# Three weight tiles move from the last attention step to the output phase, and the fills there are dealt out anew

## The chip, the core and the metric

The kernel runs on one core of a Trainium2 chip. A core has TensorE (matrix products, called PE in the profile, with its weight loads as PEld), VectorE (DVE), ScalarE (ACT), GpSimd (POOL) and SyncE (SP), which run side by side and wait for each other through semaphores; 16 DMA engines move data between HBM and the on-chip memories SBUF and PSUM. The metric is the device time of one execution in microseconds (us). The kernel is measured in repeated runs, and the median counts. Before the change it is 441.6 us (ten runs, 441.0 to 442.49).

## What is computed

Two layers. The first is an attention with feature maps instead of a softmax; the second takes its output, mixes 64 low frequencies of the sequence with complex weights, transforms back and adds a ReLU layer. In the reference, cut to what matters:

```python
def _attn_ref(q, k, v, w_phi):            # q, k, v: (8, 8, 576, 64)
    def phi(x):
        proj = np.einsum('bhsd,df->bhsf', x, w_phi)
        proj = proj - np.max(np.abs(proj), axis=-1, keepdims=True)
        return np.concatenate([np.exp(proj), np.exp(-proj)], axis=-1)
    q_p, k_p = (phi(q), phi(k))
    kv = np.einsum('bhsf,bhsd->bhfd', k_p, v)
    z = np.sum(k_p, axis=2)
    num = np.einsum('bhsf,bhfd->bhsd', q_p, kv)
    den = np.einsum('bhsf,bhf->bhs', q_p, z)[..., None] + 1e-06
    return num / den

def _moe_ref(x, w_r, w_i, w_ch):          # x: (8, 576, 512), w_r, w_i: (64, 512, 512)
    X = np.fft.rfft(x, axis=1)
    Xr, Xi = (np.real(X[:, :64]), np.imag(X[:, :64]))
    Yr = np.einsum('bmd,mde->bme', Xr, w_r) - np.einsum('bmd,mde->bme', Xi, w_i)
    Yi = np.einsum('bmd,mde->bme', Xr, w_i) + np.einsum('bmd,mde->bme', Xi, w_r)
    Y = np.zeros_like(X); Y[:, :64] = Yr + 1j * Yi
    y = np.fft.irfft(Y, n=576, axis=1)
    u = x + y
    return u + np.maximum(u @ w_ch, 0.0)
```

The weights w_r and w_i are by far the largest input: 2 x 64 matrices of 512 x 512.

## The kernel before

**Tiling.** The attention is cut into 16 units, a unit being one pair of heads g (four of them) and one pair of batches bp (four). The 512 channels of the second layer are the same four groups g of 128. The frequency weights are cut into 64 tiles: a key (g, w) names channel group g, octet o = w // 2 (eight frequencies) and i = w % 2 (w_r or w_i). A tile is 128 partitions x 4 x 2 x 512 in bf16, 1 MB on the chip, converted from float32 by the DMA. Using a tile is called a mix (function `mix`, L461): eight matmuls of 512 columns into one PSUM bank. An octet is finished by its eighth mix, over the four groups and both kinds of weights.

**Weight tiles.** `next_w` (L359) takes the next key from the list and issues its load on POOL's queue. Most tiles lie in the pool `pw` with nine buffers; a tile that is issued has to wait for the buffer that a former mix gives back. In the output phase the same pool also gives the buffers of `yall` and `zall` (and later `yl`, `rx`, `of`), which are taken when they are first written.

**Attention loop.** It starts at L504 with n from -2 to 16. Step n runs the early stages of unit n + 1 and n + 2, the main stages of unit n (called Q) and the last stage, the Fourier sums, of unit n - 1 (called P). Between these stages `some` (L488) runs mixes whose tiles are due and issues a load after each. How many mixes a step runs follows from X at L506: none before step 4, eight in step 4, three in each later step. In the last step, n = 16, there is no unit 16: Q is None, P is unit 15, and the step consists of the Fourier sums of unit 15 and three mixes.

**Output phase.** It starts at L574. The mixes that are left run in the loop at L900, each followed by `next_w(1)`. Between them `fill(n)` (L797) takes n pieces of other work from the list `todo`: 37 pieces (one opening piece and 36 calls of `hold`) that transpose a 128-row chunk of the attention output and multiply it by w_ch (the last three of them leave the product open in PSUM), then six pieces that finish these three chunks, then 33 pieces (`all`) that add the inverse transform of octets 0 to 5 to a chunk and to its product. The first of these pieces also build tables for the inverse transform on DVE and ACT. The pieces from the 38th on need octets 0 to 5 in `yall` and `zall`; A at L795 is the number of such pieces. TensorE, DVE, ACT, POOL and SP each execute their instructions in the order of the program, so the order written in this loop is the order of execution on each engine.

**When an octet is done** (g = 3, i = 1, L913), DVE adds the bank to the sum in `yacc` and writes `yst`, SP stores it into `yall`, TensorE transposes `yst`, multiplies it by w_ch (`pz`), and the result goes as `zst` to `zall`. For octets 0 to 4 one or two fills lie between these steps; for octets 5 and later the fills come behind them. After octet 7, the last, the chunks are finished and stored (class `Last`, from L811).

**How fills are dealt out.** `left` is the number of mixes still to come, and n at L912 is computed after each mix. While more than seven are left, the pieces that don't need the stored octets are spread over the mixes until seven are left; from then on, all that is left is spread over the remaining mixes. Eight are left when octet 5, the sixth, is stored.

## Time and profile before

One execution was profiled. Its own time is 441.52 us and its span, from the first to the last instruction, 439.7 us.

| what | value |
|---|---|
| median of ten runs | 441.6 us |
| profiled execution, time / span | 441.52 / 439.7 us |
| PE busy | 337.5 us (77% of the span) |
| DVE busy | 297.9 us (68%) |
| ACT busy | 278.1 us (63%) |
| POOL busy | 97.0 us (22%) |
| HBM read / written | 163.64 MB / 9.44 MB |
| mean granted TensorE clock | 0.907 of full speed |

In order of time: the attention, with mixes strewn in, runs until about 286 us; the output phase's mixes and fills follow until 404 us, and the final matmuls and stores until the end. A line of TensorE's list in order of time reads: start in us, duration, engine, operation, the tile written <- the tiles read, the sizes, how many matmuls in a row, and in brackets how long the engine was idle before and whose event ended that. `wt,XT` are mixes, `wchb,xT` the products of fills, `ident_b,xs` their transposes. Page and tables give the clock as a share of full speed, and DMA as the mean busy share of the 16 engines, where packets that overlap can bring it above 1.

### The profile page before, as it was taken

How to read it: one execution, taken by the hardware profiler on the slowest of the kernel's cores; microseconds unless marked ns; L12 is line 12 of the kernel's file. 1: busy time of each engine (PE TensorE's matmuls, PEld its weight loads, DVE VectorE, ACT ScalarE, POOL GpSimd, SP SyncE). 2: the span in 40 equal slices, each digit the busy share in tenths (PEclk: the TensorE clock that was granted, in tenths of full speed). 3: DMA queues.
4: the chain of work that ended last, by engine and by line, in shares of the span. 5: the costliest groups of instructions: out<-in, count | busy, mean ns of one | idle time of the engine just before them, and what ended most of it. 6: DMA issues, size and time to landing. Idle time of an engine off the chain costs nothing.

```text
span 439.7 us, 10163 instructions
## 1 busy us (share of the span) xinstructions
PE 337.5 (77%) x4247; PEld 203.9 (46%) x4247; DVE 297.9 (68%) x583; ACT 278.1 (63%) x478; POOL 97.0 (22%) x138
## 2 busy tenths in 40 slices
PE   3667757869777687797796785927689988999993
PEld 2345545636555455464564463613345544344320
DVE  5768588676684777866878778717763433776694
ACT  4698698677798577865877777502544432656681
POOL 7132132132221222222222121211101120010171
PEclk9989699698899689886989789987899999999996
DMA  8999999999999999999999999999999999996797
GB/s 167 236 211 210 236 214 237 232 218 240 236 211 239 220 228 236 237 212 237 225 222 238 210 239 226 225 212 212 212 216 223 219 224 221 213 217 144 244 360 297
DMA packets 51582, 99.55 MB, mean 226 GB/s; under 512 B 2512, under 2 KB 13648, under 8 KB 51536
## 3 DMA queue, kind: packets, MB, share of 16 engines
q0 software_dynamic: 45376, 86.45, 99.8%
q1 hardware_dynamic: 6160, 12.45, 8.0%
q8 instruction: 33, 0.54, 0.5%
q14 instruction: 13, 0.11, 0.1%
HBM read 163.64 MB, written 9.44 MB: 394 GB/s over the span
## 4 chain that ended last, share of the span: by engine, by line
DMA 35%; PE 34%; DVE 13%; ACT 10%; issue 5%; POOL 1%; DVEq 0%; POOLq 0%; ACTq 0%
PE one L37 12%; PE pt L37 12%; DMA vn<-in_v_dram 11%; DMA kb<-in_k_dram 10%; DMA wt<-in_moe_w_i_dram 7%; DMA wt<-in_moe_w_r_dram 7%; PE two L37 6%; PE pp L37 5%; ACT AB L37 5%; DVE m L37 3%; DVE mk L37 3%; ACT AQ L37 2%; DVE xw L37 2%; DVE xs L37 2%; ACT qT L37 1%
## 5 line engine op out<-in xcount | busy, mean ns | idle before, releaser
L37 ACT ACTIVATE AB<-two 128x1024 bf16<-128x1024 f32 x64 | 62.0, 1026 | 17.1 <-DVE mk L37 14.6
L37 ACT ACTIVATE AQ<-two 128x1024 bf16<-128x1024 f32 x64 | 62.6, 1045 | 2.6 <-PE two L37 2.5
L37 ACT CAST xw<-pt 128x512 bf16<-128x512 f32 x50 | 29.4, 587 | 45.2 <-PE pt L37 30.8
L37 DVE TENSOR_REDUCE m<-two 128x8 f32<-128x1024 f32 x32 | 39.2, 1224 | 15.1 <-PE two L37 15.0
L37 DVE TENSOR_TENSOR va<-vn,ee 128x1152 bf16<-128x1152 f32 x32 | 42.0, 1355 | 5.5 <-DMA vn<-in_v_dram 5.5
L37 DVE TENSOR_REDUCE mk<-two 128x8 f32<-128x1024 f32 x32 | 38.9, 1218 | 7.1 <-PE two L37 7.1
L37 PE MATMUL pt<-wchb,xT 128*128 128x512 bf16 x136 | 37.0, 397 | 6.6 <-DVE xT L37 5.7
L37 POOL DMA_DIRECT2D wt<-in_moe_w_i_dram x28 | 20.9, 747 | 84.3 <-PE pt L37 38.2
L37 POOL DMA_DIRECT2D wt<-in_moe_w_r_dram x30 | 22.4, 746 | 76.2 <-PE one L37 34.7
L37 PEld LDWEIGHTS <-xs 128*128 128x128 bf16 x624 | 31.7, 103 | 12.7 <-issue 7.4
L37 PE MATMUL one<-wt,XT 128*32 128x512 bf16 x304 | 27.5, 446 | 12.9 <-DMA wt<-in_moe_w_i_dram 4.3
L37 ACT COPY qT<-one 128x512 bf16<-128x512 bf16 (+1 forms) x32 | 19.3, 641 | 27.5 <-PE one L37 27.1
L37 PE MATMUL two<-w2blk,qT 128*128 128x256 bf16 x128 | 22.7, 307 | 18.0 <-ACT AB L37 8.9
L37 PEld LDWEIGHTS <-qT 128*128 128x128 bf16 x144 | 14.9, 106 | 36.5 <-issue 32.9
L37 PE MATMUL two<-qT,w2blk 128*128 128x512 bf16 x64 | 27.7, 432 | 3.5 <-ACT AQ L37 3.4
L37 PEld LDWEIGHTS <-XT 128*32 128x32 bf16 x512 | 14.7, 149 | 32.6 <-issue 16.8
L37 DVE RECIPROCAL rd<-one 128x6 f32<-128x6 f32 x48 | 9.4, 195 | 28.5 <-PE one L37 28.4
L37 PEld LDWEIGHTS <-AQ 128*128 128x128 bf16 x512 | 24.9, 109 | 7.9 <-issue 4.4
L37 PE MATMUL one<-kvz,AQ 128*128 128x65 bf16 x512 | 27.6, 209 | 1.1 <-ACT qT L37 1.0
L37 DVE TENSOR_TENSOR xs<-one,rd 128x384 bf16<-128x384 f32 x48 | 26.8, 558 | 1.6
L37 PE MATMUL two<-mT,minus 96*128 96x512 bf16 x64 | 27.5, 430 | 0.2 <-DVE mT L37 0.2
L37 PE MATMUL two<-w2blk,kT 128*128 128x256 bf16 x128 | 21.2, 294 | 8.2 <-ACT AB L37 8.2
(147 smaller groups left out, 712.4 us busy)
## 6 DMA issues: line engine op xcount, KB each, us to landing
wt<-in_moe_w_r_dram POOLq DMA_DIRECT2D x30, 1024.0 KB, 28.4
wt<-in_moe_w_i_dram POOLq DMA_DIRECT2D x28, 1024.0 KB, 29.0
vn<-in_v_dram POOLq DMA_DIRECT2D x15, 576.0 KB, 25.0
out_dram<-of SPq DMA_DIRECT2D x16, 512.0 KB, 4.6
kb<-in_k_dram POOLq DMA_DIRECT2D x16, 288.0 KB, 22.1
qb<-in_q_dram POOLq DMA_DIRECT2D x16, 288.0 KB, 21.6
xs<-in_moe_w_i_dram POOLq DMA_DIRECT2D x2, 1024.0 KB, 24.8
yacc<-in_moe_w_r_dram POOLq DMA_DIRECT2D x1, 1024.0 KB, 9.8
```

The lines of the kernel that those rows point to most:

```text
L37: ins = f(*args, **kwargs)
```

## The change

The last attention step runs no mixes any more: X becomes 0 where there is no unit Q. The three mixes, (2, 8), (2, 9) and (2, 10), are left in the list and run as the first ones of the output phase, each followed by its `next_w(1)` as before, and now with fills behind them. Their results go to a bank of the output phase's pool instead of one of the attention's.

The rule for n changes too: while more than eight mixes are left, the pieces that don't need stored octets, less four, are spread over the mixes until eight are left; when exactly eight are left, which is when the sixth octet is stored, n is four; below eight it is the old formula.

```diff
-        X = 0 if n < 4 else 6 if n == 4 else 3
+        X = 0 if n < 4 or not Q else 6 if n == 4 else 3
...
         left = len(mixq)
-        n = -(-max(len(todo) - A, 0) // (left - 7)) if left > 7 else math.ceil(len(todo) / (left - 0.4)) if left else 0
+        if left > 8:
+            n = -(-max(len(todo) - A - 4, 0) // (left - 8))
+        else:
+            n = 4 if left == 8 else math.ceil(len(todo) / (left - 0.4)) if left else 0
```

Fills per mix, as the two rules give them. Mixes are numbered 1 to 64 in the order in which they run; the mix in bold stores an octet.

| mix | 41, 42, 43 | 44, 45, **46** | 47 to **50** | 51, **52** | 53 to 55 | **56** | 57, 58, 59, **60**, 61, 62, 63 |
|---|---|---|---|---|---|---|---|
| before | none | 3 each | 3 each | 3, 2 | 2 each | 2 | 7, 7, 7, 6, 6, 6, 3 |
| after | 2 each | 2 each | 2 each | 2 each | 2 each | 4 | 7, 7, 7, 6, 6, 6, 3 |

(48 and 54 store octets as well.)

## The prediction

> **What bounds the kernel now.** I read the first page, then a table of the stretches after the attention, then TensorE in order of time from 285 us, then the weight issues on POOL's queue. I number the 64 weight tiles, and the mix that uses each, in the order of their loads: mix 44 is the first mix of the output phase before the change, mix 56 ends the sixth octet, mix 64 ends the eighth.

> ```profile
> span 439.7 us, 10163 instructions
> ...
> q0 software_dynamic: 45376, 86.45, 99.8%
> ```

> The queue that carries the weights fills the 16 engines over the whole span. The next view is a table by stretch (engine busy times, then TensorE's clock, the DMA share, GB/s):

> ```profile
> 287.00:298.00 11.00, 2.45 (x32) 0.80 (x23) 1.59 (x4) 0.53 (x2) 1.52 (x3) 0.76 1.12 212
> 298.00:321.00 23.00, 17.85 (x128) 9.56 (x120) 18.01 (x72) 10.43 (x18) 2.92 (x4) 0.82 1.12 212
> 321.00:361.00 40.00, 36.90 (x306) 19.63 (x305) 18.00 (x48) 17.06 (x33) 5.18 (x7) 1.00 1.12 221
> 361.00:378.00 17.00, 14.55 (x103) 6.88 (x102) 8.17 (x16) 5.91 (x12) 1.48 (x2) 1.00 1.12 219
> 378.00:404.00 26.00, 25.14 (x151) 9.96 (x144) 19.65 (x33) 16.13 (x31) 2.14 (x4) 1.00 1.03 204
> ```

> The DMA share is 1.12 in every stretch up to 378 us; TensorE is idle for most of 287 to 298 and all but full from 321. In TensorE's order of time (start, duration, idle before and what ended it):

> ```profile
> 292.52 1.02 PE L37 MATMUL one<-wt,XT 128*32 128x512 bf16 x8 [4.25 <-DMA wt<-in_moe_w_r_dram]
> 297.48 1.08 PE L37 MATMUL one<-wt,XT 128*32 128x512 bf16 x8 [3.93 <-DMA wt<-in_moe_w_i_dram]
> ...
> 299.99 1.89 PE L37 MATMUL pt<-wchb,xT 128*128 128x512 bf16 x4 [0.46 <-DVE xT L37]
> ...
> 361.43 0.66 PE L37 MATMUL pt<-wt,XT 128*32 128x512 bf16 x8 [0.86 <-DMA wt<-in_moe_w_i_dram]
> ...
> 364.53 1.03 PE L37 MATMUL pt<-wchb,xT 128*128 128x512 bf16 x4
> ...
> 366.80 0.66 PE L37 MATMUL pt<-wt,XT 128*32 128x512 bf16 x8 [0.16 <-DMA wt<-in_moe_w_r_dram]
> ...
> 372.62 0.67 PE L37 MATMUL pt<-wt,XT 128*32 128x512 bf16 x8 [0.29 <-DMA wt<-in_moe_w_i_dram]
> ...
> 377.57 0.66 PE L37 MATMUL pt<-wt,XT 128*32 128x512 bf16 x8 [0.24 <-DMA wt<-in_moe_w_r_dram]
> ...
> 403.60 0.66 PE L37 MATMUL pt<-wt,XT 128*32 128x512 bf16 x8
> ```

> Mixes 42, 43 and 44 (287.61, 292.52, 297.48) wait 0.37, 4.25 and 3.93 us for their weights: 8.55 us of TensorE. Then TensorE is behind until mix 56 at 361.43, which again waits for weights, as do 57, 58 and 59, each by less than a microsecond. From 377.57 the chain of waits runs on TensorE to mix 64 at 403.60 without a gap. The weights are there just as late: POOL's queue shows

> ```profile
> 333.68 0.74 POOL L37 DMA_DIRECT2D wt<-in_moe_w_i_dram  x1 [18.19 <-PE pt L37]
> ...
> 367.78 0.74 POOL L37 DMA_DIRECT2D wt<-in_moe_w_i_dram  x1 [4.64 <-PE pt L37]
> ```

> These are loads 56 and 64; the list of issues gives 27.7 and 35.5 us to landing, so they land at 361.4 and 403.3. Two equally long paths thus meet at mix 64: the DMA queue, and from mix 57 on TensorE. After it the tail of 439.7 - 403.6 = 36.1 us follows.

> [...] weights move at 212 GB/s in 298 to 321, and when SP's stores of octets join, the sum is only 221. So the order in which the two queues are fed doesn't create bandwidth. [...] two neighbouring windows in the table by stretch:

> ```profile
> 306.34:309.76 3.42, 1.40 (x12) 0.78 (x11) 2.85 (x5) 2.96 (x4) 0.74 (x1) 1.00 1.12 211
> 309.76:313.17 3.41, 3.16 (x14) 1.59 (x13) 2.31 (x5) 1.20 (x3) 0.00 (x0) 0.50 1.13 212
> ```

> A window with TensorE busy 1.40 of 3.42 us (41%) is followed by one at 0.50; the product at 299.99, in another such window, took 1.89 us against 1.03 at 364.53. The window at 361 with 2.20 of 3.40 (65%) is followed by a full one. [...]

> **The change part by part.** (1) X = 0 in the last step takes mixes 41 to 43 out of it; they come before mix 44 in the output phase. Nothing is added or dropped: 3 x 8 matmuls, three loads on POOL (loads 50 to 52), one sum into yacc on DVE move with them. The instruction order of POOL and of SP is the same as before, and so are the tiles that each load waits for: loads 50 to 55 wait for the mix nine before, from 56 on for the mix seven before, because yall and zall then hold two of the nine buffers. Load 56 waited for mix 49 before (332.70, issue 333.68) and does after.

> (2) Fills (here each a product with its transposes, plus a piece of the table building on DVE) that stood behind mixes 44 to 46 three at a time now stand behind 41 to 46 two at a time. So TensorE, which slept 8.55 us, works. It is then ahead: two products take 2 x 1.08 = 2.16 us (365.39 to 364.31 is 1.08 from one to the next), a mix 0.66, half an octet's own work about 0.75 (an estimate: some 1.5 us of TensorE between 362.62 and 364.31), together 3.6 us beside one load in 361.43 - 355.9 = 5.5 us (load 55: 314.74 + 41.2 = 355.9) or 5.0 when weights move alone. By mix 53 at the latest TensorE waits for every tile. What is this worth? Nothing at mix 56: before, it already waited there for load 56, whose landing the saturated queue sets. Load issue isn't late either: load 56 found 3 to 4 others outstanding (loads 52 to 55) and can only be issued earlier.

> (3) Up to the sixth octet 32 fills were done before mix 56 and two behind it; after, 30 before and four behind it. From mix 57 on both are the same: 42 fills left, 7, 7, 7, 6, 6, 6 and 3. So between mix 56, fixed by load 56, and mix 57 TensorE has two more products: +2.16 us. What lay free there: 0.16 us of waiting at mix 57, then 0.29 at 58 and 0.24 at 59, which the delay eats: 0.69. The waits for yst (0.53) and yT (0.19) in the octet are before the products and stay. Net 2.16 - 0.69 = 1.47 us at mix 59. From there to 403.60 TensorE has no waits that a delay can eat, and the loads 60 to 64 land earlier than needed. So mix 64 starts at 403.60 + 1.47 = 405.07, and the tail moves with it: all of it hangs on the last octet's yst, whose matmuls and DVE adds follow at once.

> (4) Small: octet 4's stores, 2 x 128 KB, were under way when load 56 landed (issues at 354.77 and 358.28, 6.4 us to land); after, they come about 4 us earlier and are through. At most half of the second, 64 KB at 212 GB/s or 0.3 us, moves ahead of load 56 and delays it; load 57 has the same bytes before it. I take 0.1, keep 0 to 0.3.

> (5) Not visible before: the clock. After mix 55 at about 356, TensorE works 0.66 + 2.16 = 2.8 us and then waits some 2.6 us for load 56. [...] If that one falls on the octet and its four products, work of up to 1.7 us becomes 3.4: between 0 and +1.7 us, by where the free windows lie; a cold window that begins before 361 covers the wait and the octet's latency-bound part, and costs less. Before, this place was safe (3.07 of 3.50 us busy in 357.5 to 361.0). The stretch from mix 57 is dense, so only one window counts. As the likeliest I take +0.4, since more than half of the positions meet the products with part of a window or none; ends 0 and 1.7.

> Sum: 1.47 + 0.1 + 0.4 = +2.0 us. Profiled: 439.7 + 2.0 = 441.7 us of span; the profiled execution's time was 441.52, and the median of the ten runs 441.6, so 441.6 + 2.0 = 443.6.

> **The rivals.** (A) Two products too many behind octet six, as above: 443.6, own range 442.7 to 445.0. For it: four mixes in a row that wait for DMA by under 0.9 us, then none that waits.

> (B) No change. The two products cost less than counted, because something else between mixes 57 and 59 gives way: for example the 0.56 us wait at 371.60 for the DVE sum into xs, or the yall landing (issue 362.92 + 6.4 = 369.3, 1.1 us ahead of its first use at 370.44), so that 2.16 - 0.69 - 0.56 = 0.9 us or less is left, and the clock stays warm: 441.6 to 442.4. Against it: that 0.56 is a wait for a PSUM bank whose releaser stands right behind on the same engines, so it moves along.

> (C) Faster: the loads land sooner. Place: the queue between 287 and 361; if its 74 us ran at 221 GB/s rather than 212 in the first 34 (octet stores begin at about 313, not 322, and deeper queues), 34 x 9 / 212 = 1.4 us; it decides only if load 56 lands more than 1.6 us sooner, since the products' delay comes off it. Were the whole stretch 4% faster, 3.0 us, mix 64 would be at 403.60 - 3.0 + 2.0 = 402.6, and the time 440.6. Against it: bytes and engines are the same, and the rate was 212 with eight loads outstanding and with four.

> (D) Much slower: cold windows repeat, since in each 5 us TensorE now waits 1 to 2.4 us from mix 45 to 56, and the first fills come while the last attention step still holds banks. The work before mix 56 has about 1.4 us of slack per load, so this shows only if it reaches mix 56 itself: a full cold window there, and one behind mix 57, about +3.5: 445.1 and more.

> **How the numbers follow.** A change of 0.2% (0.9 us) is about what a measurement of this kernel can tell from none. Chances: A 0.62, B 0.22, C 0.08, D 0.08. A's lower end at 442.7 is slower by 0.25%, so slower = A + D = 0.70; B is the same but for some of it, 0.20 after 0.02 goes to faster; faster 0.10. The likeliest, A, gives 443.6. The range leaves out C and the far part of D and of B: 441.5 to 445.0.

> **What would show it.** Right: no waits for weights left between 287 and 298 without products beside them; mix 56 at 361.4 to 361.7 after a wait of over 2 us; four products behind octet six; mix 57 at 368.7 or later with no wait for its load; mixes 58 to 64 without waits, 64 at about 405.5; a tail of 36.1 us. A clock of 0.5 in one window near 361 would add to it. Wrong: mix 56 before 360, which makes the DMA queue elastic (C); mix 57 within 0.9 us of 366.80 (B); a TensorE that still runs late at mix 56, without a wait, which would break step 2.

## The result, and the profile after

The changed kernel takes 445.12 us in the median of 12 runs, against 441.75 us of the kernel before in 42 runs alongside it: a ratio of 1.0075 with a 95% interval of 1.0064 to 1.0086. That is 3.4 us slower. The profiled execution took 445.37 us, with a span of 443.6 us, 3.9 us more than before.

TensorE's list in order of time, after the change (start, duration, idle before and what ended it):

```profile
287.10 0.62 PE L37 MATMUL pt<-ident_b,xs 128*128 128x128 bf16 x8
...
290.25 0.66 PE L37 MATMUL pt<-wt,XT 128*32 128x512 bf16 x8
...
355.73 0.66 PE L37 MATMUL pt<-wt,XT 128*32 128x512 bf16 x8 [0.93 <-DMA wt<-in_moe_w_r_dram]
...
361.83 1.08 PE L37 MATMUL pt<-wt,XT 128*32 128x512 bf16 x8 [3.17 <-DMA wt<-in_moe_w_i_dram]
...
364.35 1.89 PE L37 MATMUL pt<-wchb,yT 128*128 128x256 bf16 x8 [0.19 <-ACT yT L37]
...
366.46 1.91 PE L37 MATMUL pt<-wchb,xT 128*128 128x512 bf16 x4
...
369.61 1.03 PE L37 MATMUL pt<-wchb,xT 128*128 128x512 bf16 x4
...
371.65 0.66 PE L37 MATMUL pt<-wt,XT 128*32 128x512 bf16 x8
...
377.11 0.66 PE L37 MATMUL pt<-wt,XT 128*32 128x512 bf16 x8
...
381.88 0.66 PE L37 MATMUL pt<-wt,XT 128*32 128x512 bf16 x8
...
407.89 0.67 PE L37 MATMUL pt<-wt,XT 128*32 128x512 bf16 x8
```

The waits for weights between mixes 42 and 44 are gone: transposes and products stand there from 287.10 (with two waits for DVE, of 1.35 us and, while it builds tables, of 3.27 us). Read on to mix 56: it starts at 361.83, after 3.17 us of waiting for its weights, 0.40 us later than before (361.43), so the early work bought nothing. Then comes what costs: mix 57 starts at 371.65, against 366.80. From mix 56 to mix 57 it was 5.37 us and is 9.82 us. The waits that stood before mixes 57, 58 and 59 are gone, so 4.85 us of delay at mix 57 are 4.49 at 58 (377.11 against 372.62), 4.31 at 59 (381.88 against 377.57) and 4.29 at mix 64 (407.89 against 403.60). What follows mix 64 takes 443.6 - 407.9 = 35.7 us, against 36.1 before.

The operations in that stretch are longer, too: the mix 1.08 us and not 0.66, the first product 1.91 and not 1.03. In the profiles before and after, every stretch between two changes of the clock is a multiple of 3.41 us; a piece of that length is called a window here. The table by stretch of the changed kernel, with the four windows around mix 56 (window, length, then busy time of PE, PEld, DVE, ACT, POOL, TensorE's clock, DMA share, GB/s):

```profile
354.77:358.18 3.41, 2.48 (x24) 1.36 (x24) 1.19 (x3) 0.83 (x2) 0.74 (x1) 1.00 1.12 223
358.18:361.59 3.41, 0.48 (x3) 0.13 (x1) 0.08 (x1) 0.61 (x2) 0.00 (x0) 1.00 1.12 223
361.59:365.00 3.41, 2.45 (x16) 0.93 (x16) 1.05 (x3) 0.37 (x1) 0.74 (x1) 0.50 1.13 213
365.00:368.42 3.42, 3.42 (x17) 2.00 (x16) 0.80 (x2) 0.38 (x2) 0.00 (x0) 0.50 1.11 216
```

The wait fills the second window (0.48 of 3.41 us busy), and the third and fourth run at half clock (0.50). The DMA share is 1.11 to 1.13 in all four: the queue of weights does not run dry here, and it is TensorE that arrives late at mix 64. Load 64 is issued at 372.62 and lands 30.4 us later, at 403.0, nearly 5 us before it is used.

### The profile page after: what moved, and what is told of

It is laid out like the page before. It is cut to its first block, busy times and chain, and to the rows that moved or that the text cites. A ratio compares the mean times of both kernels' runs of the same rounds, so it can differ in the third digit from the quotient of the medians.

```text
span 443.6 us, 10168 instructions
## 1 busy us (share of the span) xinstructions
PE 342.1 (77%) x4247; PEld 205.6 (46%) x4247; DVE 298.6 (67%) x583; ACT 278.3 (63%) x478; POOL 97.1 (22%) x138
## 3 DMA queue, kind: packets, MB, share of 16 engines
q0 software_dynamic: 45376, 86.45, 98.9%
## 5 line engine op out<-in xcount | busy, mean ns | idle before, releaser
L37 ACT ACTIVATE AB<-two 128x1024 bf16<-128x1024 f32 x64 | 62.0, 1026 | 12.3 <-DVE mk L37 9.8
L37 ACT ACTIVATE AQ<-two 128x1024 bf16<-128x1024 f32 x64 | 62.7, 1045 | 2.6 <-PE two L37 2.5
L37 ACT CAST xw<-pt 128x512 bf16<-128x512 f32 x50 | 29.4, 588 | 47.0 <-PE pt L37 44.2
L37 DVE TENSOR_REDUCE m<-two 128x8 f32<-128x1024 f32 x32 | 39.2, 1224 | 17.7 <-PE two L37 17.7
L37 PE MATMUL pt<-wchb,xT 128*128 128x512 bf16 x136 | 38.4, 408 | 9.4 <-DVE xT L37 8.5
L37 DVE TENSOR_TENSOR va<-vn,ee 128x1152 bf16<-128x1152 f32 x32 | 42.0, 1355 | 3.1 <-DMA vn<-in_v_dram 3.1
L37 DVE TENSOR_REDUCE mk<-two 128x8 f32<-128x1024 f32 x32 | 38.9, 1218 | 7.6 <-PE two L37 7.6
L37 POOL DMA_DIRECT2D wt<-in_moe_w_i_dram x28 | 21.1, 752 | 85.5 <-PE pt L37 42.6
L37 POOL DMA_DIRECT2D wt<-in_moe_w_r_dram x30 | 22.4, 746 | 74.1 <-PE one L37 30.2
L37 PEld LDWEIGHTS <-xs 128*128 128x128 bf16 x624 | 32.0, 104 | 13.3 <-issue 8.2
L37 PE MATMUL two<-w2blk,qT 128*128 128x256 bf16 x128 | 23.1, 311 | 18.5 <-ACT AB L37 8.6
L37 ACT COPY qT<-one 128x512 bf16<-128x512 bf16 (+1 forms) x32 | 19.2, 641 | 27.2 <-PE one L37 26.9
L37 PEld LDWEIGHTS <-qT 128*128 128x128 bf16 x144 | 14.8, 105 | 35.4 <-issue 31.3
L37 PE MATMUL two<-qT,w2blk 128*128 128x512 bf16 x64 | 27.7, 433 | 3.4 <-ACT AQ L37 3.2
L37 PEld LDWEIGHTS <-XT 128*32 128x32 bf16 x512 | 14.5, 149 | 32.2 <-issue 19.9
L37 PEld LDWEIGHTS <-AQ 128*128 128x128 bf16 x512 | 25.3, 110 | 8.6 <-issue 5.4
L37 PE MATMUL one<-kvz,AQ 128*128 128x65 bf16 x512 | 27.7, 210 | 1.5 <-ACT qT L37 1.1
L37 PE MATMUL one<-wt,XT 128*32 128x512 bf16 x272 | 25.3, 459 | 4.3 <-DVE XT L37 2.7
L37 DVE RECIPROCAL rd<-one 128x6 f32<-128x6 f32 x48 | 9.4, 195 | 28.6 <-PE one L37 28.5
L37 PE MATMUL two<-mT,minus 96*128 96x512 bf16 x64 | 27.7, 433 | 0.2 <-DVE mT L37 0.2
L37 DVE TENSOR_TENSOR xs<-one,rd 128x384 bf16<-128x384 f32 x48 | 26.7, 557 | 1.6
L37 PE MATMUL two<-w2blk,kT 128*128 128x256 bf16 x128 | 21.3, 295 | 8.1 <-ACT AB L37 8.1
```

What stands on the lines that cost most here:

```text
L37: ins = f(*args, **kwargs)
```

## The experiments

Three theories were put to the test. T: the loss is two more products behind the sixth octet, less the waits that they eat, plus half clock behind the longer wait for load 56. R1: the clock is a bystander. R2: the moved mixes and their loads cost. All ratios are against the kernel before, run alongside, with 95% intervals. The first half of the change is the new X, the second half the new rule for n; "kept warm" means with the idle matmuls that the first experiment adds. "56 to 57" is the time from the start of mix 56 to the start of mix 57 in the profile, "half clock" the number of windows at half clock that overlap it.

| kernel | ratio | interval | 56 to 57 | half clock | mix 64 starts |
|---|---|---|---|---|---|
| before | 1 | | 5.37 us | 0 | 403.60 us |
| changed | 1.0075 | 1.0064 to 1.0086 | 9.82 | 2 | 407.89 |
| changed, kept warm | 1.0035 | 1.0026 to 1.0044 | 7.32 | 0 | 406.33 |
| first half alone | 1.0024 | 1.0012 to 1.0037 | 7.18 | 2 | 406.24 |
| first half, kept warm | 0.9994 | 0.9982 to 1.0006 | 5.15 | 0 | 403.67 |
| second half alone | 1.0070 | 1.0046 to 1.0094 | 9.98 | 2 | 408.34 |
| second half, kept warm | 1.0040 | 1.0024 to 1.0056 | 7.32 | 0 | 405.02 |
| six products, kept warm | 1.0088 | 1.0070 to 1.0107 | 9.50 | 0 | 407.60 |

**The changed kernel, kept warm.** Twelve matmuls that nobody reads fill the wait for load 56:

```diff
         else:
             fill(n)
+        if left == 9:
+            idle = bank()
+            for _ in range(12):
+                pe.matmul(idle, lhsT=ident_b, rhs=wchb[:, 0, :], start=True, stop=True)
```

> The changed kernel with 12 matmuls of 512 columns behind the products of mix 55, into a bank that nobody reads (12 x 0.216 = 2.6 us, in the 3.17 us that TensorE waits for load 56). Theory T (the delay of 4.3 us at mix 64 is two products, 2.16 us less some 0.5 us of old waits, plus about 2.4 us of half clock behind the wait): no window at half clock between 355 and 372, the octet and its four products take 7.4 us rather than 9.8 from mix 56 to mix 57, mix 57 at about 369.2, mix 64 at about 405.4, time 443.3 to 443.7, slower than before by 0.35 to 0.45%. Rival R1 (the clock is a bystander and the products and the octet themselves stall behind a late operand or bank): 9.8 us stay, time about 445.1. Rival R2 (the loss comes from the moved mixes and load issue): about 445.1 as well, with mix 56 unmoved.

Its list in order of time:

```profile
359.49 2.75 PE L37 MATMUL pt<-wchb,ident_b 128*128 128x512 bf16 x12
362.79 0.66 PE L37 MATMUL pt<-wt,XT 128*32 128x512 bf16 x8 [0.54 <-DMA wt<-in_moe_w_i_dram]
...
370.11 0.66 PE L37 MATMUL pt<-wt,XT 128*32 128x512 bf16 x8
```

and its table by stretch:

```profile
358.18:361.59 3.41, 3.41 (x20) 1.69 (x19) 0.42 (x1) 1.17 (x2) 0.25 (x1) 1.00 1.13 222
361.59:365.00 3.41, 2.11 (x18) 0.88 (x16) 1.05 (x3) 0.37 (x1) 0.74 (x1) 1.00 1.12 220
```

These stretches are cut at the changed kernel's windows. At this execution's own, 357.65 to 361.06 and 361.06 to 364.48, TensorE is busy for 3.36 and 2.31 us. The window before mix 56 is now all but full, and the octet runs at full clock (1.00); the octet's own window, no busier than in the changed kernel (2.31 us against 2.45), is followed by full clock as well. More work made the kernel faster: 1.0035 against 1.0075. That leaves no room for R1, and none for R2 in this part of the loss; whether the 0.35% that are left are the products or R2, the two halves of the change show. The mix itself came 1 us later in this execution, since load 56 landed later; such a shift of the whole stretch differs from one execution to the next, so the time from mix 56 to 57 is the better measure.

**The first half alone.** X as in the change, n by the old rule, which leaves two products behind mix 56 and gives one more each to mixes 41 and 42:

> The first half of the change alone: the three mixes go to the output phase, fills are dealt out by the old rule, which gives one more each to mixes 41 and 42 and leaves two behind mix 56. Theory T: the same wait of about 3 us before mix 56 and so the same half clock behind it, but two products fewer, one or two of them at half clock: mix 57 at 368.5 to 369.5, mix 64 at 405.0 to 406.0, time 443.2 to 444.2 (+0.3 to +0.55%). R1: as before the change in this place, so about 441.8. R2: about 445.1.

The wait for load 56 is as long (3.19 us), the clock is at half for two windows (the first begins at 361.65, before mix 56 at 362.82), and from 56 to 57 it takes 7.18 us. Mix 57 (370.00) and mix 64 (406.24) come a little later than expected, since mix 56 came a microsecond later too; the ratio, 1.0024, lies just below the expected 0.3 to 0.55%. The same with the idle matmuls:

> The first half of the change alone, with the 12 idle matmuls behind mix 55. Theory T: no half clock and no added products, so mix 57 waits for load 57 again as before the change and all that is won in 287 to 298 is lost in waits: time 441.5 to 442.1, no change against before. R1: about 441.8 as well. R2: about 445.1. A gain of more than 0.5 us would say that the loads can land earlier than the full queue allowed.

```profile
362.24 0.66 PE L37 MATMUL pt<-wt,XT 128*32 128x512 bf16 x8
...
367.39 0.66 PE L37 MATMUL pt<-wt,XT 128*32 128x512 bf16 x8
```

Here 56 to 57 takes 5.15 us, mix 64 starts at 403.67 and the time can't be told from that of before. Against the expectation, mixes 56 and 57 do not wait in this execution: TensorE had been at half clock until 355.5, and the idle matmuls ended right at mix 56. So the 5.15 us hold no wait for weights. The moved mixes cost nothing by themselves that the interval (0.9982 to 1.0006) would show, and the filled 8.55 us in front of mix 44 gain nothing: R2 falls, and so does the hope of a gain. The difference of the two kernels, 7.18 - 5.15 = 2.03 us, is half clock alone, with two products in it. In the median it is 1.0024 against 0.9994, or 1.3 us; the half clock costs less there than in the one profile.

**The second half alone.** The rule for n as in the change, X as before:

> The second half of the change alone: the last attention step keeps its three mixes, and two products move from before mix 56 to behind it. Theory T: TensorE reaches mix 56 about 2.2 us sooner than before the change, waits about 2.5 to 3 us for load 56, so the window before it is likely under half busy; +1.5 us from the products and 0 to 2.5 from the clock, by where the windows fall: time 443.3 to 445.5, likeliest 444.5. R1: about 445. R2: about 441.8, since the mixes stand where they stood.

```profile
358.18:361.59 3.41, 1.11 (x9) 0.51 (x7) 0.42 (x1) 1.17 (x2) 0.00 (x0) 1.00 1.12 222
361.59:365.00 3.41, 2.17 (x14) 0.75 (x14) 1.05 (x3) 0.37 (x1) 0.74 (x1) 0.59 1.13 220
365.00:368.42 3.42, 3.42 (x16) 1.94 (x14) 0.80 (x2) 0.37 (x1) 0.00 (x0) 0.50 1.11 215
```

These stretches of its table are cut at the changed kernel's windows; its own half clock begins at 362.2. At its own windows TensorE is busy for 0.59 us in the one before that, and for 2.70 us in the first at half clock. The second half loses as much as the whole change, without a single mix moved: two products fewer before mix 56 are a wait of 2.82 us there, where it had been 0.86. With the idle matmuls:

> The second half of the change alone, with the 12 idle matmuls behind mix 55. Theory T: only the two products are left: mix 56 to mix 57 in 7.3 us, mix 64 about 1.5 us later than before the change plus what the idle matmuls push (they take 2.75 us of a wait that was 2.82), time +0.3 to +0.45%. Rival R2 (moved products cost otherwise than through the clock and their own length): stays at +0.7%.

From 56 to 57 it takes 7.32 us, as in the changed kernel kept warm, and 1.0040 is within that one's interval.

**Six products behind the octet, kept warm.** The number of products alone is raised:

```diff
-            n = -(-max(len(todo) - A - 4, 0) // (left - 8))
+            n = -(-max(len(todo) - A - 6, 0) // (left - 8))
...
-            n = 4 if left == 8 else math.ceil(len(todo) / (left - 0.4)) if left else 0
+            n = 6 if left == 8 else math.ceil(len(todo) / (left - 0.4)) if left else 0
```

> The changed kernel with six products instead of four behind the sixth octet (mixes 54 and 55 then have one fill each) and the 12 idle matmuls behind mix 55. Theory T: two more products at full clock, nothing left to eat them: mix 56 to mix 57 takes 7.32 + 2.17 = 9.5 us, mix 64 is 2.2 us later than with four products kept warm, time 2.2 us above that kernel, so +0.85% (0.75 to 0.95) against before. Should the wait before mix 56 now be long enough for a half-clock window in spite of the idle matmuls, up to 2.5 us more. Rival R1 (products cost nothing by themselves): as with four, +0.35%.

The ratio is 1.0088, as expected. (A in these lines is 42: the 39 pieces that need the stored octets and the three that leave their product open in PSUM. So 34 pieces remain, of which 30 are spread over mixes 41 to 55 in the changed kernel, and 28 here.) From 56 to 57 it takes 5.15, 7.32 and 9.50 us with two, four and six products at full clock: a product is 1.09 us, and nothing hides it.

**Products between the octet's steps.** The fills of octet 5 are dealt like those of octets 0 to 4; `o < 5` becomes `o < 6` in the three places behind the sum, behind the transposes and behind the store:

> The changed kernel with the fills of octet 5 dealt as those of octets 0 to 4: one product between the sum and the transposes, one before the products with yT, two behind. Theory T: the 0.53 and 0.19 us in which TensorE waits for yst and yT are filled, and the half-clock window that begins at mix 56 is busy, so that the second one may not come: mix 56 to mix 57 takes 9.82 - 0.72 = 9.1 us with two windows at half clock and about 8 with one; time 443.0 to 444.6. If both windows still come: the return to full clock does not depend on the small waits.

The ratio is 1.0030 (1.0017 to 1.0043). From 56 to 57 it takes 7.81 us with one window at half clock: the octet's waits are filled, and the one half-clock window (from 363.0) is busy all through, after which full clock returned. The time is 442.6 us, 1.5 us above before (441.1 us in the same series), where the expectation, counted from 441.75, said 1.3 to 2.9. That is no slower than with the idle matmuls (1.0035, the intervals overlap), although no work was added: the same products, put into the octet's gaps, undo most of what the half clock cost.

**Fills between the steps of octets 5 and 6, first half, kept warm.** The same with `o < 7`:

> The first half of the change, the idle matmuls, and fills between the steps of octets 5 and 6, so that TensorE has some 0.7 us less to do between mixes 56 and 57 and again between 60 and 61. Theory T: mixes 57 to 59 wait for their loads, and mix 64 can't start before load 64 has landed (403.3 in the profile of before, mix 64 there at 403.60): time 0 to 0.5 us below before, not to be told from it. If TensorE alone set mix 64 after mix 59, it would be 0.7 us or more below, with mix 64 before 403.

It missed: 1.0062 (1.0049 to 1.0075). Its list shows a wait that no other kernel here has:

```profile
371.26 0.41 PE L37 MATMUL pt<-yall,CI 96*64 96x512 bf16 x2 [0.57 <-DVE xs L37]
373.64 0.38 PE L37 MATMUL pp<-zall,CI 96*128 96x512 bf16 x1 [1.98 <-DMA zall<-zst]
373.95 0.97 PE L37 MATMUL pt<-wt,XT 128*32 128x512 bf16 x8
```

The products in between push the store of zst back to 366.83 (before: 365.05), it lands 6.7 us after that, at 373.5, and TensorE, which is ahead, has reached the first matmul that reads it. The wait leaves the window with 0.96 of 3.40 us busy, and the next runs at half clock:

```profile
370.80:374.20 3.40, 0.96 (x7) 0.40 (x10) 1.60 (x3) 0.14 (x1) 0.00 (x0) 0.99 1.14 226
374.20:377.60 3.40, 3.40 (x15) 0.81 (x8) 0.14 (x1) 1.60 (x3) 0.00 (x0) 0.50 1.13 214
```

So products behind the sixth octet do have a use: they cover the 6.5 us that its last store takes. Before the change that cover was just enough (zst stored at 365.05, landed 6.5 us later at about 371.5, first read at 371.94), and two more products bought cover that nobody needed. What this run was to show, whether load 64 alone holds mix 64 back, it doesn't show, since TensorE was late again.

**The changed kernel again, twice, for its profiles.**

> The changed kernel once more, for its profile alone: does the half clock at the sixth octet depend on where the free-running windows fall? Theory T: the wait before mix 56 is again about 3 us, and the octet with its four products takes 7.3 us plus 0 to 2.5 by the windows: 9.8 us with two windows at half clock, about 8.5 with one, 7.3 with none. If it is 9.8 us whatever the windows do, the clock is not the whole of it.

> As the run before: another profile of the changed kernel, with the same expectation.

From 56 to 57 they take 8.90 and 8.74 us, each with one window at half clock, from 363.5 and from 363.6, where the first profile had two from 361.6. Mix 64 starts at 406.78 and 407.02. So the same kernel loses 1.4 to 1.6 us to the clock with one window and 2.5 with two. Where the windows fell is the difference that the three profiles show; the runs of the changed kernel spread from 443.06 to 446.36.

**Five idle matmuls instead of twelve.**

> The changed kernel with 5 idle matmuls behind mix 55 instead of 12: 1.1 us of the 3.17 us wait is filled and about 2.1 us stay idle. In the profile of before a window with 41% busy was followed by half clock and one with 65% was not. Theory T: the window that holds the wait has at least 1.3 of 3.41 us busy (38%) and at most some 60%, so half clock comes in part of the executions: time between the warm one and the changed kernel, +0.35 to +0.75%. At +0.35% or less: 2.1 us of idleness are harmless.

The ratio is 1.0044 (1.0030 to 1.0057), and the profile shows no half clock between mixes 56 and 57. But that execution is not the case that was meant: TensorE had been at half clock until 354.55 and came late, so it waited only 0.23 us before mix 56. The ratio lies between those of the changed kernel and the one kept warm, and its interval overlaps the latter's, so how much idleness is harmless isn't settled by it.

No kernel of these beats the one before; the first half kept warm can't be told from it.

## Why the prediction was right in direction and wrong in size

- **The bound (the DMA queue up to mix 56, TensorE behind it): right.** Mix 56 came at 361.83, 0.13 us past the foretold 361.4 to 361.7, after a wait of 3.17 us ("over 2"). The first half kept warm, which has all of TensorE's gain in 287 to 298 and none of the loss, is at 0.9994.
- **Step 1, moved mixes and loads cost nothing: right,** by the same run. Load 56 was issued at 326.44 instead of 333.68 and landed no sooner.
- **Step 3, +1.47 us from two products less 0.69 us of old waits: right.** Two products are 2.17 us (7.32 - 5.15), and the changed kernel kept warm is at +0.35%, 1.55 us. The old waits went as foretold: 0.16 us at mix 57 and 0.54 us (4.85 - 4.31) from there to mix 59, 0.70 in all.
- **Step 4, +0.1 us for stores that move ahead of load 56: not told apart.** Load 56 came 0.40 us later in the profile, and its use between 361.1 and 362.8 in the other kernels.
- **Step 5, +0.4 us "as the likeliest" for the clock: this term failed.** The clock cost 2.50 us in the first profile (9.82 - 7.32), 1.4 to 1.6 in the other two, and in the median 1.0075 against 1.0035, or 0.40% of 441.75: 1.8 us (some 0.6 us either way, an estimate from the two intervals). Half clock behind the wait, in this place, was forecast; that the wait would bring it was the author's estimate, from two windows of the profile before (41% and 65% busy). Two statements made its cost too small. "More than half of the positions meet the products with part of a window or none" counted a window as cheap when it lies only in part on the products. But the octet's own matmuls pay as well (those with yT took 1.89 us instead of 1.05), so the window at 363.5, with only the first product in it, still cost 1.6 us (8.90 - 7.32), near the 1.7 of the bound, an estimate of step 5. All three profiles have at least one such window whole behind mix 56; three are too few for a share. And "only one window counts" was wrong: in the first profile the window at 361.6, with the octet's waits in it (2.45 of 3.41 us busy), was followed by half clock once more. The bound of 1.7 us was the better value for one window, and the range should have reached a second one.
- **Sum.** 1.47 + 0.1 + 0.4 = 2.0 was forecast. With 1.8 for the clock it is 3.4, as measured; since the 1.8 is itself a difference of these ratios, what this confirms is the rest, 1.57 against the 1.55 of the kernel kept warm. The range ended at 445.0, just below the 445.12.
- **The rivals.** Rival B (no change) fell, rival C (loads land sooner) fell with the first half kept warm, and mix 56 starts before 361.1 in no profile. Rival D came nearest: it named a full window at half clock at mix 56 and a second one, and its 445.1 is what was measured. But it put the second window behind mix 57, where none was seen, and gave the case a chance of 0.08.

Not tried: whether the kernel before would gain if load 64 landed earlier; that mix 64 can't start before its load is read from the landing times, and no run isolates it.

## What to carry to other kernels

Before work is moved, ask what sets the time at which the engine may go on. Here it was the DMA queue, with a share of 1.11 to 1.13 around mix 56, and work that was done sooner only made the wait before mix 56 longer, 3.17 us instead of 0.86. What counted was how much was left behind the last wait: each product that the spreading rule moved there was paid in full, with 1.09 us. Add up what the longer wait does to TensorE's clock: here some 3 us of idleness right in front of the busiest stretch cost about 1.8 us in the median, as much as the two products did (1.55 us, less old waits). Before moving work away from or to a place behind a store, look at how long that store takes (6.5 us here) and whether the cover is already enough.

## What the runs showed of the hardware that had not been expected

In the changed kernel's first profile a window at half clock with 2.45 of 3.41 us busy was followed by another at half clock, and one with 3.42 us by full clock, whereas a window at full clock with 2.31 us (the changed kernel kept warm) was followed by full clock.

Waits for load 56 of 2.82, 3.17 and 3.19 us (second half alone, changed kernel, first half alone) were followed by half clock; with 12 idle matmuls of 2.75 us in such a wait, TensorE stayed at full clock.
